# Seven products for eight with w_out also in the first eight tiles of batches 0 to 2, and PSUM in single banks

## The chip, the core and the metric

The kernel runs on one core of a Trainium2 chip. The time is the device time of one execution in microseconds. PE is TensorE's matmul side and PEld its weight loads, DVE is VectorE, ACT is ScalarE, POOL is GpSimd, SP is SyncE, which here only issues DMAs. Each engine works off its own list of instructions in order and waits for others at semaphores.

## What is computed

A long convolution with a gate, then a feed-forward network with a maxout of three (B = 4 batches, S = 12544 positions, D = 128 channels, 768 hidden). Cut to what matters:

```python
h_filt = np.maximum(pos_emb @ w1, 0) @ w2 * window          # (S, D)
u = x * v                                                   # (B, S, D)
y = irfft(rfft(u, 2*S, axis=1) * rfft(h_filt, 2*S, axis=0), axis=1)[:, :S]
t = (x * y).reshape(B * S, D)                               # 50176 tokens
h = np.maximum(np.maximum(t @ moe_w1, t @ moe_w2), t @ moe_w3)
out = h @ moe_w_out
```

All of it is in fp32; each fp32 matmul shows as two MATMUL rows in the profile.

## The kernel before

**Tiles and batches.** S = 128 x 98. A tile is 4 x 98 = 392 tokens, a batch has 32 tiles (NT). The hidden 768 are 6 blocks of 128 (NF), so that a batch's FFN has 192 steps, one for each tile and block. The kernel has four parts: the prologue to about 303 us (the filter's spectrum, the weights, batch 0's forward and inverse transform); the FFNs of batches 0 to 2, each with the next batch's convolution done beside it; the FFN of batch 3, beside which nothing is left to convolve (from about 1860 us on); and the drain.

**The FFN.** `w1` and `w2` are held less `w3`, so that the maxout is `max(relu(a), b)` of two products plus a linear part `lin = w3 @ w_out`. `up` (L721) makes one hidden block of a tile: two products into two of the three banks `hps` (each in two halves of 64 output channels, `halves_mm` at L156), ACT's relu (L727) and DVE's max (L730). `down` (L733) adds that block's product with `w_out` into the bank `ops`, with the product of `lin` first when f is 0; after the sixth block ACT copies the bank (L743) and POOL issues the store (L745). In the loop over tiles a down runs two steps behind its up.

**A tile's input.** `t_load` (L661) has SP fetch the tile's transform (`zt`, four DMAs) and, for every second tile, x (`xT`, four DMAs). `t_sums` (L687) makes a sum and a difference (L696), on POOL while units are in work and on DVE otherwise. `t_last` (L703) does the last transform stage on the PE, in one bank, and DVE multiplies with x (L717); its result `gt` is what the ups read.

**The convolution beside.** `conv_steps(b, done)` plans, for each of the 192 steps, what is added behind the up and the down. First come the 32 units: loads by SP (`u_load`), x * v on DVE (`u_mul`, L361), planes of 16 bit on POOL (`u_planes`, L381 and L382), a transposing DMA issued by SP (`u_dma`, L388), a join on ACT and DVE (`u_join`, L397), and the first transform stage (`u_first`, L413): 32 matmul rows into a double bank, a copy of one half by ACT (`high`, L422) and a sum and a difference by DVE (`spec`, L424). For a unit due at step s these stand at steps s-9, s-6, s-5, s-4, s and s+1; units follow each other every 1.52 steps, and the last are due near step 55 (batch 0) or 62. Then come 45 + 3 quarters: loads by SP (`w_load`, `q_load`, `h_load`), the PE's second and third stages (`g_quarter`, L467 and L477) in one double bank, the copy and sums out of it (`g_fold`, L489 and L492), and the products with the filter's spectrum on ACT, DVE and POOL.

**PSUM.** Eight banks: three `hps`, two double banks `cps` that go round among units, quarters and the turns of tiles (`t_last`), and one `ops`.

**The last batch.** Tiles go in pairs. A pair is taken as a 2 x 2 block product: two tiles (c11 and c12 belong to the first, c21 and c22 to the second) by the two halves of the 768 hidden and the two halves of `w_out`'s 128 columns, and seven products do for eight. A pair has 12 ups, in an order of its own (`ORDER`), the sums s1 to s4 of hidden blocks on POOL (`sum_`, L760, 12 of them of 128 x 392), and seven products (`products`, L790) of which each instruction covers 64 output channels by 196 columns, in two banks X and Y that change places from pair to pair. The results come out by ACT copies and DVE sums (L807) into an `o` tile, and POOL issues its eight stores (L814). Products run nine steps behind the ups (LAG). Five subtractions on DVE (L1175) make the combinations of `w_out` and `lin` that the products use; they stand at the start of the last batch, and one of them overwrites b12 of `w_out`. The order within each engine is the program's own.

Of the kernel before, what the change touches and what calls it, by code (L numbers as in the profile page):

```python
# [91 lines left out]
def kernel(  # L92
# [311 lines left out]
    def u_first(u, i0=0, n=4):  # L404


        t = uts[u] if i0 + n < 4 else uts.pop(u)
        ps = state["bank"]()[:, 0:256 * n]
        at = 4 * u + i0
        for i in range(n):  # L410
            for h in range(2):
                for c in range(2):
                    nc.tensor.matmul(  # L413
                        ps[64 * c:64 * c + 64, 256 * i + h * N1:256 * i + (h + 1) * N1],
                        t[:, 2 * ((at + i) % 8) + h].rearrange("n r t -> n (r t)"),
                        f1q[:, h, c * N1:(c + 1) * N1],
                        start=(i % 2 == 0 and h == 0), stop=True, skip_group_check=True)
        v = ps.rearrange("p (s m) -> p s m", m=256)[:, :, 0:2 * N1].rearrange(
            "p s (h k) -> p h k s", h=2)
        high = cvp.tile([P, n, D], FP32, tag="eo", name="high", bufs=2)  # L420
        high = high[:, :, 0:N1].rearrange("p s k -> p k s")
        nc.scalar.copy(high, v[:, 0])  # L422
        for a, op in enumerate((ALU.add, ALU.subtract)):
            nc.vector.tensor_tensor(out=spec[:, :, a, at:at + n], in0=v[:, 1], in1=high, op=op)  # L424

# [31 lines left out]
    def g_quarter(g, z):  # L457


        ps = state["bank"]()  # L460
        if g is not None:
            w, t = ws.pop((g, 0)), sqs.pop(g)
            for k in range(2):
                for r in range(2):
                    for a in range(2):
                        at = 512 * r + k * D
                        nc.tensor.matmul(  # L467
                            ps[64 * a:64 * a + 64, at:at + D], w[64 * r:64 * r + 64, k, a, :],
                            t[64 * r:64 * r + 64, k, a, :], start=(k == 0), stop=True,
                            skip_group_check=True)  # L470
        if z is not None:
            w, ab = ws.pop((z, 1)), abs_.pop(z)
            for q in range(2):
                for a in range(2):
                    for k in range(2):
                        at = 512 * a + 256 + q * D
                        nc.tensor.matmul(  # L477
                            ps[64 * k:64 * k + 64, at:at + D], w[64 * a:64 * a + 64, k, q, :],
                            ab[64 * a:64 * a + 64, q, k, :], start=(g is None and q == 0),
                            stop=True, skip_group_check=True)  # L480
        pss[g, z] = ps

    def g_fold(g, z):
# [5 lines left out]
        nc.scalar.copy(eo[:, lo:hi], ps[:, 512 + lo:512 + hi])  # L489
        cb = cvp.tile([P, 2, 512], FP32, tag="cb", name="cb", bufs=3)  # L490
        for a, op in enumerate((ALU.add, ALU.subtract)):
            nc.vector.tensor_tensor(out=cb[:, a, lo:hi], in0=ps[:, lo:hi], in1=eo[:, lo:hi],  # L492
# [84 lines left out]
    def conv_steps(b, done):  # L577
# [9 lines left out]
        for u in range(4, done):  # L587
            at(2 * u - 7, 1, u_first, u)
        per_pair = 170 / (NK + LATE + 0.6 * (NU - done))
        for u in range(done, NU):  # L590
# [6 lines left out]
            at(int(s + 1), 1, u_first, u)  # L597
# [29 lines left out]
        for x in range(NK + LATE):  # L627
# [4 lines left out]
            at(s - 4, 0, w_load, x)  # L632
# [4 lines left out]
            if g % 2 == 0:  # L637
                at(s - 4, 0, q_load, g, min(2, NK - g))
# [19 lines left out]
    NT = P // 4  # L658
    zts, xTs, gs, pos_, obs = ({} for _ in range(5))
# [43 lines left out]
    def t_last(i):  # L703
        zt = zts.pop(i)
        ps = state["bank"]()
        own = i[0] == B - 1 and i[1] > 1
        g = (lp if own else hp).tile([D, 4, NB], FP32, tag="g", name="gt", bufs=4 if own else 3)
# [14 lines left out]
    def up(i, f, tag="hid", bufs=3):  # L722
        rhs = gs[i][:].rearrange("d p n -> d (p n)")
        h = (hidp if tag == "hid" else lp).tile([P, N], FP32, tag=tag, name="hid", bufs=bufs)
# [8 lines left out]
    def down(i, f, h):  # L733
        if f == 0:
            pos_[i] = ops.tile([D, 512], FP32, tag="ops", name="ops")
# [26 lines left out]
    def s3(h, j):  # L762
        h["s3", j] = lp.tile([P, N], FP32, tag="s3", name="s3", bufs=3)
        sum_(h["s3", j], h["h11", j], h["h21", j], ALU.subtract)

    def s2(h, j):
        h["s2", j] = lp.tile([P, N], FP32, tag="s2", name="s2", bufs=3)
# [5 lines left out]
    def s4(h, j):  # L773
        sum_(h["h12", j], h["h12", j], h["s2", j], ALU.subtract)

    SUMS = {2: (s3, 0), 4: (s2, 0), 5: (s3, 1), 7: (s3, 2), 8: (s2, 1), 9: (s2, 2),
            10: (s1, 0), 11: (s1, 1), 12: (s1, 2), 13: (s4, 0), 14: (s4, 1), 15: (s4, 2)}

    def products(b, i, h, X, Y):
# [5 lines left out]
        def new(name, bufs=1):  # L785
            return lp.tile([P, H2], FP32, tag=name, name=name, bufs=bufs)
# [6 lines left out]
        def place(name):  # L793
# [5 lines left out]
            if m not in t:  # L799
                t[m] = lp.tile([P, 2, H2], FP32, tag="o", name="o", bufs=2)  # L800
# [8 lines left out]
        def stored(m):  # L809
            dst = outT.rearrange("d (p b n) -> d p b n", b=B, n=NB)  # L810
            for n in range(2):
                for c in range(2):
                    at = 4 * (i + n) + 2 * c
                    nc.gpsimd.dma_start(  # L814
# [8 lines left out]
            (X, "h21", wo_sb[:, 0:NC, 64:128], True, None, [(added, "c22", "u3", X)], None),  # L823
# [16 lines left out]
    def run(steps):  # L840
        for fn, args in steps:
            fn(*args)

# [112 lines left out]
    state = {"cv": (cvp, cps), "xb": 2, "bank": bank,  # L956
# [69 lines left out]
    def unit(u):  # L1026
        for h in range(2):
            u_first(u, 2 * h, 2)

# [52 lines left out]
    nc.sync.dma_start(sign_t[:], sign_d)  # L1082
    op_ = ctx.enter_context(tc.tile_pool(name="op", bufs=2))
    conv = ExitStack()
    inq = conv.enter_context(tc.tile_pool(name="inq", bufs=1))
    wp = conv.enter_context(tc.tile_pool(name="wp", bufs=3))
    hh = conv.enter_context(tc.tile_pool(name="hh", bufs=2))
    cvp = conv.enter_context(tc.tile_pool(name="cvp", bufs=3))
    hps = ctx.enter_context(tc.tile_pool(name="hps", bufs=1, space=PSUM))
    cps = conv.enter_context(tc.tile_pool(name="cps", bufs=1, space=PSUM))  # L1090
    ops = conv.enter_context(tc.tile_pool(name="ops", bufs=1, space=PSUM))
    hbanks = itertools.cycle([hps.tile([P, 512], FP32, name=f"hps{i}") for i in range(3)])
    pairs = itertools.cycle([cps.tile([P, 1024], FP32, name=f"cps{i}") for i in range(2)])
    state = {"bank": lambda: next(pairs)}
# [5 lines left out]
    for n, (b, i) in enumerate(tiles[:LAST]):  # L1100
        if i == 0:
            beside, plan, pairs_from = conv_steps(b + 1, EARLY if b == 0 else 0)
        if n == 0:
# [3 lines left out]
            u_first(2)  # L1107
            t_last(tiles[0])
            u_first(3)
        for f in range(NF):  # L1110

            if i < NT - 2:
                if f == 0:
                    t_load(*tiles[n + 2])
            elif i == NT - 1 and f < 2 and n + 1 + f < len(tiles):
                t_load(*tiles[n + 1 + f])
            turn_ = i == NT - 1
            if f == 4 and n + 1 == LAST:
                t_sums(tiles[n + 2], nc.vector)
            h = up((b, i), f)  # L1120
            for a in range(2):
                if f == plan[i][a]:
                    t_sums(tiles[n + 1],
                           nc.vector if turn_ or i * NF > pairs_from else nc.gpsimd, (a,))
            late.append(((b, i), f, h))
            if len(late) > 2:
                down(*late.pop(0))
            if f == plan[i][2]:
                t_last(tiles[n + 1])
            if f == 5 and n + 1 == LAST:  # L1130
                t_last(tiles[n + 2])
            s = i * NF + f
            run(beside.pop(s, ()))
            if s == NT * NF - 1:
                assert not beside, sorted(beside)
    first = up((B - 1, 0), 0)
    for l in late:
        down(*l)
    conv.close()


    lp = ctx.enter_context(tc.tile_pool(name="lp", bufs=1))
    cps = ctx.enter_context(tc.tile_pool(name="cps2", bufs=1, space=PSUM))
    singles = itertools.cycle([cps.tile([P, 512], FP32, name=f"last{i}") for i in range(3)])
    state = {"bank": lambda: next(singles)}
# [3 lines left out]

    tw = lp.tile([P, 3, NC, 64], FP32, name="tw", bufs=1)  # L1150
    linx = lp.tile([D, 64], FP32, name="linx", bufs=1)
    b11, b12 = wo_sb[:, 0:NC, 0:64], wo_sb[:, 0:NC, 64:128]
    b21, b22 = wo_sb[:, NC:, 0:64], wo_sb[:, NC:, 64:128]
    weights = [(tw[:, 1], b22, b12), (b12, b12, b11), (tw[:, 0], b22, b12),
               (tw[:, 2], b21, tw[:, 0]), (linx[:], lin[:, 0:64], lin[:, 64:128])]

    stream = {}

    def later(step, fn, *args):
        stream.setdefault(step, []).append((fn, args))  # L1160

    step, b = 0, B - 1
    for i in range(0, NT, 2):
        h = {}
        X, Y = banks if i % 4 == 0 else banks[::-1]
        for j, (name, f) in enumerate(ORDER):
            n = int(name[1]) - 1
            if j < 2 and i + 2 < NT:
                t_load(b, i + 2 + j)
            own = (name, BUFS[name]) if step > 2 else ("hid", 3)  # L1170
            h[name, f] = first if step == 0 else up(
                (b, i + n), f + (NC if name[2] == "2" else 0), *own)
            if step > 2 and weights:
                out, a1, a2 = weights.pop(0)
                nc.vector.tensor_tensor(out=out, in0=a1, in1=a2, op=ALU.subtract)  # L1175
            if j == 0:
                entries = products(b, i, h, X, Y)
                for q, e_ in enumerate(entries):
                    at_ = step + LAG + q * NSTEP // len(entries)
                    for fn in e_:  # L1180
                        if isinstance(fn, tuple):
                            later(at_ + 1, *fn)
                        elif fn is not None:
                            later(at_, fn)
                for at_, (fn, c) in SUMS.items():
                    later(step + at_, fn, h, c)
# [45 lines left out]
```

## Time and profile before

| | |
|---|---|
| runs | 2292.55, 2300.68, 2299.49, 2294.06 us; median 2296.78 |
| profiled execution | 2292.55 us, of which the span from the first to the last instruction is 2290.7 |
| granted TensorE clock | 0.999 |
| matmul rows of `up` (392 columns) | 6144 |
| matmul rows of `down` with `w_out` (392 columns) | 2304 |
| POOL sums of hidden blocks, L760 | 192, all in the last batch |
| SP's transposing DMAs, L388, in the profile | 90 |

The page gives busy time by engine, the share of the span in 40 slices, the DMA queues, the chain of work that ended last, and the costliest groups of instructions with what ended the idle time before them. Where a helper issues an instruction, its line is the helper's: ups, downs, lin and turns of tiles are all L156, and are told apart by the names of their tiles (`hps<-gt,w_sb` an up, `ops<-hid,wo_sb` a down, `ops<-gt,lin`, `cps<-f4p,even` a turn). In the timeline a row is a run of like instructions: start, duration, engine, line, operation, tiles, form and count; what stands in brackets is the idle time before it and what ended it. By stage (busy us in windows of the span):

| window, us | what runs | PE | DVE | ACT | POOL |
|---|---|---|---|---|---|
| 845 to 980 | batch 1, units beside | 135.0 of 135 | 94.1 | 62.6 | 56.8 |
| 1000 to 1180 | batch 1, quarters beside | 178.3 of 180 | 141.6 | 115.8 | 56.6 |
| 1900 to 2260 | batch 3, pairs, no convolution | 360.0 of 360 | 173.0 | 91.9 | 233.7 |

### The profile page before, as it was taken

To read this page: it belongs to the slowest core of one execution; us is meant where nothing else is said; L and a number is where in the kernel's file an instruction comes from. 1 tells how busy PE (TensorE), PEld (TensorE's weight loads), DVE (VectorE), ACT (ScalarE), POOL (GpSimd) and SP (SyncE) were. 2 spreads that over 40 slices of the span, in tenths; PEclk is the share of its full clock that TensorE was granted. 3 is DMA by queue.
4 is the path that set the end of the run, shared out by engine and by line. 5 is a ranking of instruction groups with operands and counts; after the bars stand their busy time and mean duration, and the time that the engine had idled before them with its cause. 6 is when DMAs were issued, how large, how long until landed. Compare 5 with 4: busy or idle time off the path is not lost.

```text
span 2290.7 us, 68538 instructions
## 1 busy us (share of the span) xinstructions
PE 2259.0 (99%) x27855; PEld 1372.9 (60%) x27855; DVE 1556.0 (68%) x2848; ACT 1175.7 (51%) x2124; POOL 874.8 (38%) x1093
## 2 busy tenths in 40 slices
PE   8999989999999999999999999999999999999998
PEld 7999856655555556655555556655555556666665
DVE  5588857667878747758887847758887854545443
ACT  2688834456666534456666624446666622222222
POOL 2044423323333234423333324323333326666666
PEclk9999999999999999999999999999999999999999
DMA  7779979799999669969999769969999832222221
GB/s 190 179 238 277 293 166 186 142 216 235 236 238 232 168 147 186 190 153 249 249 236 248 198 129 198 185 148 236 250 252 248 212 86 55 55 66 66 62 55 22
DMA packets 473270, 411.03 MB, mean 179 GB/s; under 512 B 327866, under 2 KB 374427, under 8 KB 472955
## 3 DMA queue, kind: packets, MB, share of 16 engines
q1 hardware_dynamic: 445954, 329.48, 64.7%
q0 software_dynamic: 26288, 75.47, 11.3%
q8 instruction: 219, 3.59, 0.7%
q10 hardware_dynamic: 712, 1.70, 0.3%
q14 instruction: 97, 0.79, 0.1%
HBM read 262.84 MB, written 84.67 MB: 152 GB/s over the span
## 4 chain that ended last, share of the span: by engine, by line
PE 90%; DMA 4%; DVE 3%; issue 1%; ACT 1%; SPq 0%; POOL 0%; DVEq 0%; POOLq 0%; ACTq 0%
PE hps L156 41%; PE ops L156 17%; PE ops L790 6%; PE cps L413 5%; PE cps L156 3%; PE ps L156 3%; PE cps L467 3%; PE ps L165 3%; PE cps L477 2%; PE sps L1000 2%; PE gps L982 1%; DMA wt<-wq_const 1%; PE last L156 1%; DVE xs L523 1%; DMA hd<-ht 1%
## 5 line engine op out<-in xcount | busy, mean ns | idle before, releaser
L156 PE MATMUL hps<-gt,w_sb 128*64 128x392 f32 x6144 | 1148.8, 494 | 0.0
L727 ACT ACTIVATE hid<-hps 128x392 f32<-128x392 f32 x768 | 384.1, 500 | 724.5 <-PE hps L156 709.7
L156 PEld LDWEIGHTS hps<-gt,w_sb 128*64 128x64 f32 x6144 | 427.9, 137 | 423.9 <-issue 395.8
L730 DVE TENSOR_TENSOR hid<-hid,hps 128x392 f32<-128x392 f32 x768 | 428.2, 558 | 341.3 <-PE hps L156 336.1
L156 PE MATMUL ops<-hid,wo_sb 128*64 128x392 f32 x2304 | 479.0, 492 | 0.0
L519 POOL TENSOR_TENSOR cb<-cb,xs 128x512 f32<-128x512 f32 x135 | 174.4, 1292 | 471.3 <-DVE xs L516 352.1
L156 PEld LDWEIGHTS ops<-hid,wo_sb 128*64 128x64 f32 x2304 | 170.0, 137 | 209.2 <-issue 209.2
L424 DVE TENSOR_TENSOR spec<-cps,high 128x360 f32<-128x360 f32 x188 | 141.3, 792 | 127.3 <-ACT high L422 127.3
L492 DVE TENSOR_TENSOR cb<-cps,eo 128x512 f32<-128x512 f32 (+1 forms) x288 | 175.2, 649 | 72.0 <-ACT eo L489 72.0
L745 POOL DMA_DIRECT2D out_dram<-ot x96 | 75.1, 783 | 367.5 <-ACT ot L743 312.6
L507 ACT ACTIVATE xs<-cb 32x512 f32<-32x512 f32 x270 | 169.6, 628 | 19.7 <-DVE cb L492 10.9
L508 ACT COPY xs<-cb 32x512 f32<-32x512 f32 x270 | 166.3, 616 | 3.2
L422 ACT COPY high<-cps 128x360 f32<-128x360 f32 x94 | 75.1, 799 | 164.5 <-PE cps L413 135.7
L523 DVE TENSOR_TENSOR xs<-cb 128x256 f32<-128x256 f32 x270 | 147.8, 594 | 10.9 <-POOL cb L519 10.9
L413 PEld LDWEIGHTS cps<-f1q,uT 98*64 98x64 f32 x3008 | 131.7, 138 | 31.8 <-issue 31.0
L413 PE MATMUL cps<-f1q,uT 98*64 98x90 f32 x3008 | 135.3, 242 | 1.3 <-DVE spec L424 0.5
L382 POOL COPY planes<-ut 128x784 uint16<-128x784 uint16 x90 | 75.8, 842 | 119.0 <-DVE ut L361 118.9
L500 POOL DMA_DIRECT2D zd<-cb x135 | 93.0, 691 | 50.5 <-DVE cb L492 47.4
L156 PEld LDWEIGHTS cps<-f4p,even 90*64 90x64 f32 x1568 | 89.8, 138 | 37.0 <-issue 33.5
L156 PE MATMUL cps<-f4p,zt 90*64 90x49 f32 x1568 | 97.2, 222 | 0.4 <-DVE zt L696 0.4
L156 PE MATMUL cps<-f4p,even 90*64 90x49 f32 x1568 | 95.9, 220 | 1.5 <-DVE even L696 1.5
L814 POOL DMA_DIRECT2D out_dram<-o x128 | 77.6, 611 | 51.7 <-DVE o L807 49.5
(134 smaller groups left out, 3130.0 us busy)
## 6 DMA issues: line engine op xcount, KB each, us to landing
ht<-hd SPq DMA_DIRECT2D x264, 256.0 KB, 7.0
wt<-wq_const SPq DMA_DIRECT2D x144, 256.0 KB, 6.7
zd<-cb POOLq DMA_DIRECT2D x135, 256.0 KB, 6.5
zt<-zd SPq DMA_DIRECT2D x384, 90.0 KB, 3.1
sq<-spec SPq DMA_DIRECT2D x264, 128.0 KB, 7.2
ut<-in_xr_dram SPq DMA_DIRECT2D x128, 196.0 KB, 4.3
ut<-in_vr_dram SPq DMA_DIRECT2D x128, 196.0 KB, 4.5
xT<-in_x_dram SPq DMA_DIRECT2D x256, 98.0 KB, 3.7
```

The costliest lines, as they stand in the source:

```text
L156: nc.tensor.matmul(out[64 * h:64 * h + 64], lhsT[:, 64 * h:64 * h + 64], rhs, start=start, stop=stop, skip_group_check=True)
L413: nc.tensor.matmul(ps[64 * c:64 * c + 64, 256 * i + h * N1:256 * i + (h + 1) * N1], t[:, 2 * ((at + i) % 8) + h].rearrange("n r t -> n (r ...
L424: nc.vector.tensor_tensor(out=spec[:, :, a, at:at + n], in0=v[:, 1], in1=high, op=op)
L492: nc.vector.tensor_tensor(out=cb[:, a, lo:hi], in0=ps[:, lo:hi], in1=eo[:, lo:hi], op=op)
L500: nc.gpsimd.dma_start(zd[b][2 * z:2 * z + 2].rearrange("k c t a f -> (k c t) a f"), zss.pop(z))
L507: nc.scalar.mul(xs[at:at + 32], xt[at + 32:at + 64], -1.0)
L508: nc.scalar.copy(xs[at + 32:at + 64], xt[at:at + 32])
L519: nc.gpsimd.tensor_tensor(out=xts[g], in0=xts[g], in1=xs[:], op=ALU.add)
L523: nc.vector.tensor_tensor(out=ab[:, q], in0=y[:, 0], in1=y[:, 1], op=(ALU.subtract, ALU.add)[q])
L727: nc.scalar.activation(h[:], pa[:, 0:N], Relu)
L730: nc.vector.tensor_tensor(out=h[:], in0=h[:], in1=pb[:, 0:N], op=ALU.max)
L790: nc.tensor.matmul(ps[64 * c:64 * c + 64, 0:H2], w, rhs[:, H2 * c:H2 * c + H2], start=start, stop=True, skip_group_check=True)
```

## The change

**Pairs in batches 0 to 2.** The first eight tiles (TP) of each of these batches are done as four pairs, with the ups, sums and products of the last batch, beside the units. The fourth pair (`ends`) has its product entries drawn together, from step 3 on after the lag, so that the stage ends near step 52. From tile 8 on, steps are as before. While pairs run no `down` is issued in steps 2 to 8 of a batch. Their stores are issued by SP instead of POOL, two steps after the results (one, in the fourth pair); the last batch's stay on POOL. `t_load`, `t_sums` and `t_last` of the pairs' tiles get places of their own, the sums of tiles 2 to 7 on POOL; in batch 0 tile 1's sums are on DVE ahead of the loop and its turn is in step 0. The tile after next is loaded and turned in a batch's last tile.

**Memory.** A pool `stp` holds the hidden blocks and sums of the pairs until their stage ends; only then are the pools of the quarters' `w`, `sq` and `h` opened, so that `w_load` and `q_load` are held back to step 52 (LOADS).

**The weights' combinations** now lie in a `tw` of four matrices, b12 is no longer overwritten, and the five subtractions stand in steps 1 to 5 of batch 0.

**PSUM.** Instead of two double banks there are four single ones (`singles`). While pairs run three of them go round, and the fourth and `obank` (the former `ops`) are the pairs' X and Y; afterwards all four go round, and `obank` is the bank of the downs again. A unit is done in two halves of one bank each; a quarter takes two single banks; a turn of a tile takes one single bank instead of a double one. Tile 8's downs begin in `obank` at step 50.

```diff
+    def unit(u):
+        for h in range(2):
+            u_first(u, 2 * h, 2)
...
-        ps = state["bank"]()
+        ps = [state["bank"]() for _ in range(2)]
...
-            at(int(s + 1), 1, u_first, u)
+            at(int(s + 1), 1, unit, u)
...
-            at(s - 4, 0, w_load, x)
+            at(max(s - 4, LOADS), 0, w_load, x)
...
+    TP = 8
+    LOADS = TP * NF + 4
...
-            pos_[i] = ops.tile([D, 512], FP32, tag="ops", name="ops")
+            pos_[i] = obank
...
-                    nc.gpsimd.dma_start(
+                    sp["store"].dma_start(
...
-            (X, "h21", wo_sb[:, 0:NC, 64:128], True, None, [(added, "c22", "u3", X)], None),
+            (X, "h21", tw[:, 3], True, None, [(added, "c22", "u3", X)], None),
...
+    def down_pair(b, i, h, banks, step, ends, wait):
+
+        entries = products(b, i, h, *banks)
+        for q, e_ in enumerate(entries):
+            at_ = q * NSTEP // len(entries)
+            if ends:
+                at_ = min(at_, 3 + (q > 8) + (q > 13) + (q > 20))
+            at_ += step + LAG
+            for fn in e_:
+                if isinstance(fn, tuple):
+                    later(at_ + wait, *fn)
+                elif fn is not None:
+                    later(at_, fn)
+        for at_, fn, c in SHORT if ends else SUMS:
+            later(step + at_, fn, h, c)
...
+    obank = cps.tile([P, 512], FP32, name="ops")
+    singles = [cps.tile([P, 512], FP32, name=f"cps{i}") for i in range(4)]
+    turn_of = {"at": 0, "of": 4}
...
+    sp = {"hid": ("h11",), "store": nc.sync}
...
+            turns_.close()
+            sp["pool"] = turns_.enter_context(tc.tile_pool(name="stp", bufs=1))
+            turn_of["of"] = 3
...
+            s = i * NF + f
             turn_ = i == NT - 1
...
+            if i < TP:
+                i0, j = i - i % 2, i % 2 * NF + f
+                if j == 0:
+                    h = {}
+                    ends = i0 + 2 == TP
+                if j in (0, 6 if ends else 4):
+                    t_load(b, i0 + 2 + (j > 0))
+                up_pair(b, i0, h, j)
+                if late:
+                    down(*late.pop(0))
+                if n == 0 and f == 0:
+                    t_last(tiles[1])
+                elif weights:
+                    out, a1, a2 = weights.pop(0)
+                    nc.vector.tensor_tensor(out=out, in0=a1, in1=a2, op=ALU.subtract)
+                if j == 0:
+                    banks = (obank, singles[3])
+                    down_pair(b, i0, h, banks if i0 % 4 == 0 else banks[::-1], s, ends,
+                              1 if ends else 2)
...
+            if i < TP and not ends:
+                if j in (3, 7):
+                    t_sums((b, i0 + 2 + (j > 3)))
...
+            run(stream.pop(s, ()))
...
+            if i < TP and not ends:
+                if j in (7, 10):
+                    t_last((b, i0 + 2 + (j > 7)))
...
+            if i >= TP and turn_of["of"] == 3 and not stream:
+                turns_.close()
+                wp = turns_.enter_context(tc.tile_pool(name="wp", bufs=3))
+                hh = turns_.enter_context(tc.tile_pool(name="hh", bufs=2))
+                turn_of["of"] = 4
             run(beside.pop(s, ()))
```

## The prediction

> **What bounds the kernel now.** I read, in this order, the page's busy shares and chain, the waits of the PE in the three batches that have a convolution beside them, the PE's timeline in both kinds of FFN, the busy time by stage, and the rows of the operations that the change touches.
>
> ```profile
> span 2290.7 us, 68538 instructions
> PE 2259.0 (99%) x27855; PEld 1372.9 (60%) x27855; DVE 1556.0 (68%) x2848; ACT 1175.7 (51%) x2124; POOL 874.8 (38%) x1093
> PE 90%; DMA 4%; DVE 3%; issue 1%; ACT 1%; SPq 0%; POOL 0%; DVEq 0%; POOLq 0%; ACTq 0%
> ```
>
> The PE is busy 99% of the span, and 90% of the chain that ended last is PE. From the start of batch 0's FFN to the end of batch 2's (303 to 1860 us) the PE waited 10.5 us in all; the largest entry in its list of waits (total, times, longest) is
>
> ```profile
> PE cps L467 <- DVE gt L717: 6.9, 8, 0.9
> ```
>
> So PE work taken out comes off the time as long as the other engines keep up. What a product costs is read from the PE's timeline, in batch 0 and in the last batch:
>
> ```profile
> 702.98 1.49 PE L156 MATMUL hps<-gt,w_sb 128*64 128x392 f32 x8
> 704.30 0.83 PE L156 MATMUL ops<-hid,wo_sb 128*64 128x392 f32 x4
> 704.96 0.50 PE L156 MATMUL hps<-gt,w_sb 128*64 128x392 f32 x2
> ```
>
> ```profile
> 2104.97 1.49 PE L156 MATMUL hps<-gt,w_sb 128*64 128x392 f32 x8
> 2106.28 0.83 PE L790 MATMUL ops<-hid,wo_sb 128*64 128x196 f32 x8
> 2106.95 1.49 PE L156 MATMUL hps<-gt,w_sb 128*64 128x392 f32 x8
> ```
>
> From start to start, four instructions of 392 columns take 0.66 us and eight of 196 columns 0.67. Averaged over long undisturbed windows I get 164.6 ns for one of 392 and 82.9 ns for one of 196.
>
> **The products (a gain).** A tile has 6 downs and one lin, 7x4 = 28 instructions of 392 columns; a pair 56x164.6 ns = 9.22 us. With seven products a pair has 21 product entries and 4 lin entries of four rows each, 100x82.9 ns = 8.29 us. That is 0.93 us a pair, and 12 pairs (4 in each of batches 0 to 2): **-11.1 us**.
>
> **Moved weights and single banks (small gains).** The five subtractions leave the start of the last batch, where two turns of the PE waited 0.31 and 0.40 us for DVE behind them: **-0.7**. In batch 0 they lie on DVE in steps 1 to 5 (214 to 705 ns each), beside units 4 and 5, in time that DVE has idle (30% in the stage below); without that cover they would cost the 0.7 again. Nine waits of the kind shown above, 7.7 us together, come where the second quarter of a slot wants the double bank that the turn of a tile holds until gt. With singles it still gets that bank as its second one and waits for it some instructions later; I count 0.1 us for each, **-0.8**, with the ends 0 and -7.7. A unit in halves has the same matmuls. Its copies and sums change by these rows (min/median/max):
>
> ```profile
> L422 ACT COPY high<-cps x94: 768/797/816, 303.9 to 1515.5; 128x360 f32<-128x360 f32 x94
> L422 ACT COPY high<-ps x4: 472/495/513, 290.4 to 296.0; 128x180 f32<-128x180 f32 x4
> L424 DVE TENSOR_TENSOR spec<-cps,high x188: 761/792/822, 305.9 to 1517.1; 128x360 f32<-128x360 f32 x188
> L424 DVE TENSOR_TENSOR spec<-ps,high x8: 334/336/347, 293.1 to 296.8; 128x180 f32<-128x180 f32 x8
> ```
>
> ACT gains 2x495-797 = 0.19 us of work a unit, DVE loses 2x792-4x336 = 0.24. Neither sets the pace there:
>
> ```profile
> 845.00:980.00 135.00, 135.00 (x1742) 84.84 (x1740) 94.08 (x165) 62.61 (x109) 56.79 (x81) 1.00 1.08 184
> ```
>
> That is the stage of units: PE 135 of 135 us, DVE 94 (70%), ACT 63 (46%), POOL 57 (42%). Cost nothing; if ACT's idle half were gone it would be 78x0.19 = 15 us.
>
> **The wait for obank (a cost).** Tile 8's first lin goes into obank, which the last pair's products used; the matmul stands in the PE's order behind ups, and it waits for the DVE sum c21. Behind it on the PE are all later ups, and so ACT and DVE too. L807's sum of 128x196 takes 0.353 us; a wait on gt of 0.563 us cost 0.82, so 0.26 lies around an operation; DVE is 70% busy, and a sum or max ahead of it takes 0.3 to 0.8 us. I take 0.8 (ends 0.3 and 1.4), three batches: **+2.4**.
>
> **Batch 0's start (a cost).** Pairs need both tiles at once: tile 1's turn is put in step 0 and its gt is wanted by step 1, with nothing else for the PE. Tile 0's start shows the price, waits of 1.50, 0.40 and 0.55 us, of which the first is
>
> ```profile
> 305.26 0.32 PE L156 MATMUL cps<-f4p,even 90*64 90x49 f32 x4 [1.50 <-DVE even L696]
> ```
>
> I take the sum of those three for tile 1, rounded: **+2.5** (0.5 if DVE's two sums are ready, 4 if ACT's and DVE's halves of units are in their way).
>
> **The starts of batches 1 and 2 (a cost).** No down runs in steps 2 to 8 of a batch, so a step takes 1.32 us instead of 1.98, and the units' first loads, 4.5 us to landing, have 7x0.66 = 4.6 us less before slot 10. The work comes back at the end of the stage; what is lost is only where a unit is late: **+2** for both (0 to 4).
>
> **POOL, SP and the rest of the stage (a cost).** A pair brings 12 sums to POOL and takes away two stores:
>
> ```profile
> L760 POOL TENSOR_TENSOR s<-hid,s x48: 1015/1027/1039, 1874.4 to 2274.1; 128x392 f32<-128x392 f32 x48
> L388 SPq DMA_TRANSPOSE turned<-planes x90: 1231/1284/3398, 322.1 to 1498.1; - x90
> DMA to landing us min/median/max: 3.1/4.4/7.6
> ```
>
> 12x1.02-2x0.78 = 10.7 us in some 36 us of a pair: POOL goes from 42% to about 73%. Its planes for a unit (0.84 and 0.30 us), which the transpose on SP waits for, stand behind one or two sums, 1.0 to 2.0 us. SP gets 8 stores a pair, at 0.45 us like its other loads 3.6 us: 65% to about 77% of its queue. Behind them stand transposes, behind these the join on ACT and DVE, behind that the relu of the next up, and the PE. The cover is the time between a turned tile's landing and its join: from the 90 landings and joins, 0.8 us at the least, 3.1 at the twentieth part, 6.3 in the middle. With 1 to 2 us from POOL and 1.8 (four stores) from SP most units stay covered. I take **+1.5**; ends 0 (all covered) and 16, worked out below. The stores' landing is waited for by nobody soon: the o tile has two turns.
>
> A rule of the Trainium skill speaks against the sums: "SBUF — State Buffer", section "Who interferes with whom", has a DVE instruction with two SBUF inputs contend with a GpSimd instruction that reads SBUF, one holding the shared port until it ends. The trace is divided: L397's copy on DVE has a median of 455 ns and a longest of 1356, while L361's product of two SBUF tiles is 558 in the median, though one of it took 1405. By the rule the two L361 products of 78 units, blocked half a sum (0.5 us) in a third of cases, would cost 26 us of DVE time, as an estimate; by the medians nothing; DVE's idle 30% would take it either way.
>
> **The sum.** -11.1-0.7-0.8+2.4+2.5+2+1.5 = -4.2, on a span of 2290.7 with 1.85 us around it (profiled run 2292.55). That run is the fastest of four, 4.2 us under the median of 2296.78; a rerun has no reason to repeat it, so I put the change on the median: **2292.6 us**. About 0.3%, 6.9 us, is what a measurement of this kernel can tell from no change; this lies inside it.
>
> **Rivals.** *A, the PE stays fed.* Loads were issued early and the singles turn quickly: then the starts cost 0.5 and 0, the stage nothing, and the sum is -11.1-0.7-0.8+2.4+0.5 = -9.7: **2287.1**. For it: a wait of PE on anything but gt is rare before. Against it: batch 0's gaps for tile 0 are in the trace. *B, slower: SP's bursts make the joins late.* A burst is four stores, 1.8 us, in one slot, before that slot's transpose; 8 bursts a batch, 6 beside units, 18 in all, up to 18x1.8 = 32 us, if the cover is gone. It decides from where POOL's delay before the planes plus the burst passes the middle cover of 6.3 us, which needs some four sums in a row ahead of planes; half of the bursts in full is +16, so 2292.6+16 = **2308.6**. For it: the transposes already wait on SP up to 3.2 us behind planes. Against it: the cover at the twentieth part, 3.1, is nearly what one burst and one sum take. *C, the products don't get cheaper beside units*: excluded by 82.9 against 164.6 ns, unless halves of width 196 meet a late operand there; 12x8.29x0.1 = 10 us for a tenth, which would end near 2302. I count it with B.
>
> **Chances.** Forecast 0.37, A 0.35, B and C 0.28. The range of the forecast alone: low all costs at their lower ends (+0.9+0.5+0+0 for +2.4+2.5+2+1.5, so 7 below, 2285.6), high +1.8+1.5+2+3 above, 2300.9. The whole range takes A's lower end with part of the nine waits gone (2284) and B a little past half of its price (2312). Faster by over 0.3% 0.35, within 0.37, slower 0.28.
>
> **What will show it.** Products: L790's rows beside units at 83 ns and the last batch the same length. Obank: a wait of lin's matmul on DVE c21 of about 0.8 us, once a batch. Starts: PE gaps in the first 10 us of each batch. B: ACT's join or high as the releaser of ups, joins close on landings, and PE waits on ACT hid or DVE hid in steps 9 to 52. The prediction is wrong if the PE waits more than some 15 us beside the pairs, or if the second quarter's wait goes entirely (-7).

## The result, and the profile after

The changed kernel takes 2303.09 us in the median of 31 runs, the kernel before 2297.6 in 51: a ratio of 1.0022, 95% interval [1.0015, 1.0028]. It is slower by some 5 us where -4.2 was forecast. Both lie inside the 0.3% that the forecast called no change, on opposite sides of zero. The page of the changed kernel:

```profile
span 2303.1 us, 70310 instructions
PE 2259.3 (98%) x28383; PEld 1423.1 (62%) x28383; DVE 1606.2 (70%) x3102; ACT 1203.6 (52%) x2218; POOL 1019.4 (44%) x1207
PE 62%; DMA 10%; DVE 2%; POOL 2%; SPq 2%; issue 1%; ACT 0%; POOLq 0%; DVEq 0%; ACTq 0%
```

PE's share of the chain went from 90% to 62%: other engines now set when the PE goes on, in many short steps. PE's busy time is no smaller although there are fewer columns to do: ends of matmuls are modelled, and part of the waiting and of a slower clock counts as busy. The waits of the PE from 303 us to the end of batch 2's FFN (total, times, longest):

```profile
PE cps L472 <- DVE gt L728: 5.3, 8, 0.7
PE cps L413 <- DVE uT L397: 3.3, 7, 1.0
PE hps L156 <- DVE hid L741: 2.7, 3, 1.1
PE cps L413 <- DVE spec L425: 2.5, 2, 2.0
...
PE cps L802 <- POOL s L771: 1.5, 2, 0.7
PE ops L156 <- DVE o L819: 1.4, 3, 0.5
PE cps L472 <- DMA wt<-wq_const: 1.2, 3, 0.6
```

All entries together are 22 us, where the kernel before had 11. The wait of second quarters has shrunk (6.9 to 5.3); new are units whose join (uT) or sums (spec) are late, ups that wait for a max, products that wait for POOL. The stage of units, which before had POOL at 57 and DVE at 94 of 135 us:

```profile
845.00:980.00 135.00, 131.73 (x1826) 100.16 (x1824) 107.54 (x237) 69.95 (x136) 106.44 (x122) 1.00 1.03 188
```

POOL is at 79% (forecast 73%), DVE at 80% where I had left its 70%, and the PE has 3.3 us idle where it had none.

Time from one landmark to the next, read off the PE's timeline at the starts of ups, in two profiles of each kernel (the second of each, and the singles, are experiments below), tells where the time went. Step 56 of a batch is just behind its pairs.

| from, to (us) | before | before, again | singles, no pairs | singles, again | changed | changed, again |
|---|---|---|---|---|---|---|
| start to first up | 309.9 | 312.5 | 312.7 | 308.2 | 311.9 | 311.7 |
| batch 0, to step 56 | 160.8 | 162.0 | 160.8 | 159.6 | 162.2 | 160.6 |
| to batch 1's step 56 | 517.5 | 517.5 | 517.4 | 517.4 | 520.7 | 522.4 |
| to batch 2's step 56 | 520.4 | 521.7 | 520.2 | 520.1 | 526.9 | 526.9 |
| to batch 3's first up | 358.3 | 358.0 | 357.5 | 357.8 | 358.8 | 357.5 |
| batch 3, to its last up | 408.3 | 408.3 | 407.5 | 407.5 | 407.3 | 407.3 |

The first three rows of the FFN each hold four pairs, and should have become 3.7 us shorter. They lie between 1.4 us shorter and 6.5 longer. Batch 0's row moves by itself: some profiles begin it with the end of a stretch in which the granted clock is 0.50 (up to 316.1 us, 3.6 us of the row, in the second profile of before), others don't (the second ones of the singles and of the changed kernel).

### The profile page after: what moved, and what is told of

It is laid out like the page before. It is cut to its first block, busy times and chain, and to the rows that moved or that the text cites. A ratio compares the mean times of both kernels' runs of the same rounds, so it can differ in the third digit from the quotient of the medians.

```text
span 2303.1 us, 70310 instructions
## 1 busy us (share of the span) xinstructions
PE 2259.3 (98%) x28383; PEld 1423.1 (62%) x28383; DVE 1606.2 (70%) x3102; ACT 1203.6 (52%) x2218; POOL 1019.4 (44%) x1207
## 4 chain that ended last, share of the span: by engine, by line
PE 62%; DMA 10%; DVE 2%; POOL 2%; SPq 2%; issue 1%; ACT 0%; POOLq 0%; DVEq 0%; ACTq 0%
PE hps L156 33%; PE ops L156 11%; PE ops L802 7%; PE cps L413 3%; DMA zt<-zd 3%; PE cps L156 2%; DMA ht<-hd 2%; PE cps L472 2%; DMA wt<-wq_const 2%; PE cps L482 2%; DMA sq<-spec 2%; PE last L156 1%; PE cps L802 1%; DVE xs L528 1%; POOL s L771 1%
## 5 line engine op out<-in xcount | busy, mean ns | idle before, releaser
L741 DVE TENSOR_TENSOR hid<-hid,hps 128x392 f32<-128x392 f32 x768 | 428.4, 558 | 351.5 <-PE hps L156 341.7
L156 PE MATMUL ops<-hid,wo_sb 128*64 128x392 f32 x1728 | 357.6, 492 | 0.0
L156 PEld LDWEIGHTS ops<-hid,wo_sb 128*64 128x64 f32 x1728 | 124.3, 137 | 159.1 <-issue 159.0
L756 POOL DMA_DIRECT2D out_dram<-ot x72 | 56.6, 786 | 287.6 <-ACT ot L754 231.9
L423 ACT COPY high<-cps 128x180 f32<-128x180 f32 x188 | 91.8, 489 | 150.7 <-PE cps L413 95.8
L425 DVE TENSOR_TENSOR spec<-cps,high 128x180 f32<-128x180 f32 x376 | 109.1, 339 | 42.9 <-ACT high L423 41.0
L771 POOL TENSOR_TENSOR s<-hid 128x392 f32<-128x392 f32 x84 | 95.6, 1139 | 78.7 <-DVE hid L741 52.5
L361 DVE TENSOR_TENSOR ut<-ut 128x392 f32<-128x392 f32 x128 | 90.1, 704 | 31.8 <-DMA ut<-in_vr_dram 28.9
L771 POOL TENSOR_TENSOR s<-hid,s 128x392 f32<-128x392 f32 x84 | 90.8, 1082 | 41.3 <-DVE hid L741 41.0
```

The costliest lines, as they stand in the source:

```text
L156: nc.tensor.matmul(out[64 * h:64 * h + 64], lhsT[:, 64 * h:64 * h + 64], rhs, start=start, stop=stop, skip_group_check=True)
L741: nc.vector.tensor_tensor(out=h[:], in0=h[:], in1=pb[:, 0:N], op=ALU.max)
L771: nc.gpsimd.tensor_tensor(out=out[:], in0=a[:], in1=b[:], op=op)
```

## The experiments

Ratios are to the kernel before, run on the same chip, with 95% intervals; the changed kernel's is 1.0022.

**Single banks without pairs (e1_singles, and e14_singles_again).** The whole change but the pairs.

```diff
-    TP = 8
-    LOADS = TP * NF + 4
+    TP = 0
+    LOADS = 0
...
```

> No pairs in batches 0 to 2: all their tiles go as before, with the stores on POOL, but PSUM in single banks, units in halves and the weights' subtractions in batch 0, as in the changed kernel. All theories agree that the losses of the changed kernel lie in the stage of pairs: they expect 2 to 4 us under the kernel before (0.999 to 0.998), from the waits of second quarters (9 x 0.2 us and more) and the last batch's 1 us. A rival, that single banks or halves are what costs, expects this run 5 us or more above the kernel before.

Measured: 2290.97 us, 0.9976 [0.9966, 0.9987], and once more 2290.33 us, 0.9968 [0.9956, 0.9981]. Single banks, halves and moved weights are together a gain, 6 to 7 us, larger than any theory had it (which of the three gives it wasn't tested); the pairs are worth +11 to +13 us. The profiles account for about half of the gain: from the first up to batch 3's last, the singles' two take 3.4 us less than the two of before in the mean, of which nine second quarters are 0.2 us each and batch 3 is 0.8 us. The rest is open.

**No sums on POOL (e2_no_sums).**

```diff
     def s1(h, j):
+        if sp["store"] is nc.sync:
+            return
```

The like stands in s2, s3 and s4.

> The 12 sums of hidden blocks per pair on POOL are left out in batches 0 to 2: the products read the hidden blocks without them, so that the output of those tiles is another. Lock theory (POOL's sums hold up DVE's copy of a join, 455 ns before and 668 to 1138 in the middle now, and take POOL's time from the planes): the waits of the PE on units, some 9 us, and part of the two starts go; 8 to 11 us under the changed kernel, 0.997 to 0.998 of the kernel before. Queue theory (SP's stores are what makes joins late): 0 to 3 us under the changed kernel.

Measured: 2291.46 us, 0.9979 [0.9968, 0.9991], 10 us under the changed kernel. Of the join's copies on DVE, here are the rows of the changed kernel and then of this one (min/median/max):

```profile
L397 DVE COPY uT<-turned x90: 446/826/3126, 333.4 to 1523.7; 98x512 uint16<-98x512 uint16 x90
```

```profile
L397 DVE COPY uT<-turned x90: 445/453/1544, 331.4 to 1511.8; 98x512 uint16<-98x512 uint16 x90
```

The copy took 455 ns before, 826 beside sums, and 453 again without them. That is the lock that the lock theory supposes, shown by taking away its cause. The products x * v on DVE (L361), which I had looked at for it, kept their median (558, 559, 559), and that median hides the same lock: of the 90 beside the FFNs, the changed kernel has 41 that overlap no sum or difference of POOL, at 539 to 569 ns, and 49 that do, at 938 in the mean and up to 3150. In the kernel before only 3 of the 90 met one. DVE's maxes (L741), which read one operand from PSUM, took 543 to 565 ns whether they met one or not. The 10 us are not the lock alone, for without the sums POOL's queue is shorter too.

**No stores of pairs (e3_no_stores).**

```diff
         def stored(m):
+            if b < B - 1:
+                return
```

> The stores of the pairs in batches 0 to 2 are left out, so that the output of those tiles isn't written. Queue theory (bursts of four stores, 2.6 us on SP's queue, make transposes late, and these the joins): the PE's waits on units go, 6 to 10 us under the changed kernel. Lock theory: 0 to 3 us under it.

Measured: 2293.73 us, 0.9987 [0.9978, 0.9996], 8 us under the changed kernel: what queue theory expected. SP's queue in the changed kernel:

```profile
1403.31 2.67 SPq L826 DMA_DIRECT2D out_dram<-o  x4
1406.15 3.70 SPq L388 DMA_TRANSPOSE turned<-planes  x2
1409.90 0.59 SPq L354 DMA_DIRECT2D ut<-in_xr_dram  x1
1410.53 1.44 SPq L354 DMA_DIRECT2D ut<-in_vr_dram  x1
1412.02 2.57 SPq L826 DMA_DIRECT2D out_dram<-o  x4
1414.63 0.59 SPq L354 DMA_DIRECT2D ut<-in_xr_dram  x1
```

SP has next to no gap here, and four stores take 2.6 us, not the 1.8 that I had worked out. The loads behind them are late as well: from 303 to 1530 us DVE waited 1.9 us for loads of v before, 14.5 in the changed kernel and 2.3 without stores. The time between a turned tile's landing and its join, 6.3 us in the middle and 3.1 at the twentieth part before, was 5.2 and 0.4 in the changed kernel, 6.0 and 1.3 without stores. Both theories hold, then: either edit alone takes most of the loss away. That a join late by one cause has no cover left for the other would explain it, and is argued, not shown.

**Both copies of a join on ACT (e4_join_act).**

```diff
-            copies[h](
+            nc.scalar.copy(
```

> Both copies of a join are on ACT, none on DVE; 0.77 us more for ACT a unit, 0.67 us or more less for DVE. Lock theory: the join no longer waits for POOL's sums, and the PE's waits on DVE's uT go (3.3 us in the profile), with some of those on the sums of units behind it: 3 to 6 us under the changed kernel. Queue theory: within 2 us of it, since late transposes make the joins as late on ACT; a loss of 2 us or more if ACT's longer join holds up relus.

Measured: 2297.73 us, 1.0002 [0.9992, 1.0012], 4.6 us under the changed kernel, the expected size. The waits on DVE's uT (3.3 us) are gone; those on spec are 4.2.

**The two kernels once more (e5_before_again, e6_after_again).**

> The kernel before once more, unchanged, for a second profile. The run with single banks alone was 6 us under it, of which its profile explains some 3 (second quarters, the last batch). If the rest is the state of the one profile of before (the fastest of its runs), a second profile lies 2 to 5 us above 2290.7, in the prologue or in waits of the PE on units; if it repeats the first within 1 us, the double banks cost something that the profile doesn't show.

> The changed kernel once more, unchanged. Waits at fixed places (starts of batches 1 and 2, tile 8's lin, batch 0's first quarters) repeat within 0.3 us each; those on units move, and with them the stretch of halved clock.

Measured: spans of 2295.6 and 2301.8 us. The profile that I predicted from was one with a quick prologue (2.6 us of the difference) and no waits on the quarters' loads, of which the second has 1.0 us. In the changed kernel the spacing of matmuls at the starts of batches 1 and 2 exceeds the normal by 1.29 and 0.89 us, at tile 8 by 0.61, as in the first to 0.02; the units' waits moved: those on spec grew from 2.5 to 5.1 us, those on DVE's uT fell from 3.3 to 1.3.

**Stores on ACT (e7_stores_act), and with both join copies on ACT (e8_stores_and_join_act).**

```diff
-    sp = {"hid": ("h11",), "store": nc.sync}
+    sp = {"hid": ("h11",), "store": nc.scalar}
```

> The pairs' stores of batches 0 to 2 are issued by ACT instead of SP; the lock by POOL's sums stays. If SP's queue is the cause, the time falls as far as without stores, less what ACT's issues (8 a pair) cost: 5 to 9 us under the changed kernel (0.998 to 1.000 of the kernel before). If the stores' traffic and not their place in SP's queue was the cost, within 2 us of the changed kernel.

> Stores on ACT and both copies of a join on ACT: both mended causes at once. If queue and lock are two causes that add up, 10 to 14 us under the changed kernel (0.996 to 0.998); if they are one (a join is late by one or the other), no further than the better of the two alone, 6 to 9 us.

Measured: 1.0005 [0.9996, 1.0014] and 0.9983 [0.9974, 0.9993]. The first is 4 us under the changed kernel, half of what leaving the stores out gave; how much of the other half is ACT's time and how much the transfers', it doesn't tell. Together they give 9 us. That is what was expected of one cause, but also the sum of the two edits alone (3.9 and 4.6), since the first gave less than expected: this pair of runs doesn't decide it.

**Early loads (e9_loads_early).** This run and those behind it build on e8.

```diff
+            if done or u > 2:
+                at(max(0, int(s) - 9), 0, u_load, b, u)
...
+                if turn_ and f > 2 and b + 2 < B:
+                    u_load(b + 2, f - 3)
```

> As the run with stores and both join copies on ACT, and the loads of the first three units of batches 1 and 2's convolution partners are issued in the last three steps of the batch before. In that run the PE still waits about 1.3 us for DVE and 0.7 us for POOL's sum some 15 us into batches 1 and 2, where DVE sits behind a unit's product whose load is late. If the short steps 2 to 8 outrun the loads, the 1.3 us go in both batches: 2 to 3 us less (0.9970 to 0.9975 of the kernel before). If SP or the planes hold the units at the start, they stay, and the time is the same within 1 us.

Measured: 0.9981 [0.9972, 0.9990], 0.4 us less than the run before it, and the 1.3 us stay. These lines show why, of SP, POOL and DVE in this run's timeline:

```profile
829.66 1.75 SPq L680 DMA_DIRECT2D zt<-zd  x4
840.58 0.40 SPq L354 DMA_DIRECT2D ut<-in_xr_dram  x1
```

```profile
838.19 1.35 POOL L772 TENSOR_TENSOR s<-hid,s 128x392 f32<-128x392 f32 x1
...
839.72 0.83 POOL L382 COPY planes<-ut 128x784 uint16<-128x784 uint16 x1
```

```profile
844.73 1.15 DVE L361 TENSOR_TENSOR ut<-ut 128x392 f32<-128x392 f32 x1 [2.48 <-DMA ut<-in_vr_dram]
845.79 1.02 DVE L742 TENSOR_TENSOR hid<-hid,hps 128x392 f32<-128x392 f32 x2
```

SP is idle from 831.4 us: the next load waits for its buffer, which the planes of an earlier unit release. These stand on POOL behind sums of tiles and of hidden blocks and end at 840.55; the load goes out at 840.58. DVE reaches that unit's product too early, waits 2.48 us in front of it, and two maxes stand behind.

**All places (e10_all_places), stores apart (e11_stores_apart), products later (e12_products_later).** In e10 the fourth pair's last entries stand ahead of tile 8's lin, and batch 0's start is reordered; e11 puts the second four stores a step later and the first units' x * v a step later; e12 does the latter for all units.

```diff
-                at_ = min(at_, 3 + (q > 8) + (q > 13) + (q > 20))
+                at_ = min(at_, 3 + (q > 8) + (q > 13))
...
-                    later(at_ + wait, *fn)
+                    later(at_ + wait + (ends and fn[1]), *fn)
...
-            at(int(s) - 6, 0, u_mul, u)
+            at(int(s) - 5, 0, u_mul, u)
```

> As the run before it, with two more places mended: the last four product entries of the fourth pair stand one step earlier, ahead of tile 8's lin, so that other matmuls cover the DVE sum that lin waits for (0.61 us in each of three batches); and in batch 0 tile 1's sums stand ahead of unit 3, and units 4 and 5 one step earlier, so that a unit covers tile 1's gt (0.58 and 0.85 us waits there). By the waits 2.5 to 3.5 us less than the run before it. If the products' gain is all there and only the listed waits are left, it ends 6 to 9 us under the run with single banks alone less what units still cost: 0.995 to 0.9965 of the kernel before.

> As the run with all places mended, whose eight stores of a fourth pair came in one step and held ACT for 6.1 us and the PE for 2 to 3.4: now the second four stand a step behind the first. In batches 1 and 2 the products x * v of the first eight units stand a step later on DVE, behind another max, so that DVE no longer waits there for a late load. If the eight stores are what that run lost by, its waits at steps 51 and 52 go and the 1.3 us at the starts too: 8 to 11 us under it (0.995 to 0.997 of the kernel before), under the run with single banks alone. If the mended places only move the wait, it stays above 0.998.

> The same with the products x * v of all units a step later. If late loads hold DVE throughout the stage of pairs (14.5 us of DVE's waits in the changed kernel), 1 to 2 us less than the run with the first eight alone; if the slack between landing and join is what is short, 1 to 3 us more, with waits of the PE on ACT's uT.

Measured: 1.0029 [1.0019, 1.0039], 0.9986 [0.9977, 0.9994], 0.9977 [0.9967, 0.9988]. In e10 the waits on lin and the first ones at batch 0's start went, and a larger one came, three times; the timeline of ACT, with its queue, then of the PE:

```profile
976.40 6.08 ACTq L827 DMA_DIRECT2D out_dram<-o  x8
982.53 1.40 ACT L397 COPY uT<-turned 98x512 uint16<-98x512 uint16 x2 [5.64 <-DMA out_dram<-o]
```

```profile
983.98 1.86 PE L413 MATMUL cps<-f1q,uT 98*64 98x90 f32 x32 [3.39 <-ACT uT L397]
```

Eight stores in one step hold ACT for 6 us, and the join behind them. Apart, the waits there are 0.7 us at most, and e11 is 9.9 us better, though not under the singles. e12 is 2.1 us better still, a step that the intervals don't separate; DVE's waits for loads of v fell from 12.6 to 2.7 us, so the late loads did hold DVE.

**Tile sums on DVE (e13_tile_sums_dve).** e12 still had 4.3 us of PE waiting for POOL's sums, 1.8 at a time in batches 1 and 2, where a tile's sums stand ahead of the hidden blocks'.

```diff
-                    t_sums((b, i0 + 2 + (j > 3)))
+                    t_sums((b, i0 + 2 + (j > 3)), nc.vector if b and i0 == 0 and j == 7 else nc.gpsimd)
```

> As the run with all products x * v a step later, and in the first pair of batches 1 and 2 tile 3's sums are on DVE instead of POOL, where they stood just ahead of two sums of hidden blocks. If POOL's queue is what the second product of these pairs waits for (1.8 us, twice), those waits go and the profiled time after the first up falls by 3 to 4 us; 0.9955 to 0.9965 of the kernel before, 3 us under the run with single banks alone. If DVE is then late instead (it locks against POOL's sums), the time stays within 1.5 us.

> The run with single banks and no pairs once more, on the same chip as the run before it, to compare the two directly: 0.997 to 0.9985 of the kernel before.

Measured: 0.9965 [0.9951, 0.9979], 2289.59 us, beside 0.9968 for the singles on the same chip. The POOL wait is gone (4.3 to 0.6 us), but 1.4 us of waiting for DVE's max came back, and the profiled time after the first up fell by 1.7 us, half of the expected. Where the rows of the table above hold pairs, this run has 158.0, 516.0 and 518.6 us, 4.5 in all under the singles' second profile, taken beside it: 4.5 us of the 11.1 are out. (Under the first it would be 5.8, but that one has 2.3 us at half clock in batch 0's row.) That the whole run is better than the singles by as much isn't shown; the medians lie 0.7 us apart, inside the intervals, and the time before the first up alone varied from 308.2 to 314.8 us between profiles.

## Why the prediction was wrong, point by point

**Products: right.** Rows of 196 columns beside units came at 83 ns from start to start, and the work taken out is the 11.1 us.

**Weights, halves and banks: right in kind, too small.** Second quarters waited 1.8 us less (forecast 0.8) and batch 3 took 1.0 less (0.7). The whole part was -6 to -7 us, not -1.5, of which the profiles explain half. This miss hid a part of the other: with -1.5 the changed kernel would have ended near 2308 us, about where rival B put it.

**The wait for obank: right.** 0.61 us by start-to-start spacing, three times, 1.8 instead of 2.4. The PE's timeline at tile 8 of batch 0:

```profile
458.18 0.88 PE L156 MATMUL ops<-gt,lin 128*64 128x392 f32 x4 [0.45 <-DVE o L819]
```

**Batch 0's start: right.** Its gaps, 0.58, 0.85 and 0.66 with smaller ones, are some 2.3 us (2.5), and some 3 in the second profile.

**Starts of batches 1 and 2: mechanism partly right, price too low.** 1.28, 0.88 and 0.38 us in each, 5.0 for 2. I had the loads late because steps are short. e9 shows for the first of the three that POOL's sums in front of the planes are the reason, by way of a buffer. The second is a product that waits for POOL's sum itself, and went with the tile sums in e13.

**POOL, SP and the rest of the stage: the step that failed.** "I take +1.5" came to some 12 to 15. By the table the changed kernel takes 12.7 us more than the singles from batch 0's first up to batch 3's, though 11.1 us of work are out: 23.8 us of delay, of which 1.8 are the wait for obank, 2.3 batch 0's start and 5.0 the starts of batches 1 and 2; 14.7 are left. The PE's timeline shows where. Between 316 and 1866 us the spacing of matmuls, start to start, exceeds what the same matmuls usually take by 19 us more in the changed kernel than in the singles, if the larger delays alone are counted (22 to 23 with the small ones): 8.1 of it ahead of units' matmuls (0.7 at the starts), 4.6 ahead of ups, 2.3 ahead of quarters, 1.8 each at tile 8 and ahead of products that wait for POOL. Less tile 8's and the starts' that is 12.

Rival B had a part of the mechanism, SP's bursts. The point from which it decides was set too high: I let a delay count only from the middle cover, 6.3 us, while the twentieth part of the units had 3.1 or less, and one burst with a sum or two takes that up; four stores took 2.6 us instead of 1.8; and the delays do not stay on one queue. SP late makes the load late (e3), DVE stands in front of its product, and the maxes behind it are late too. The sign that I had named, over 15 us of waiting beside the pairs, came: some 21 us by the spacing.

The place where it is dearest shows the last term that the sum lacked. The timelines of DVE, then of the PE, in the changed kernel:

```profile
1462.57 1.30 DVE L397 COPY uT<-turned 98x512 uint16<-98x512 uint16 x1
1466.18 0.57 DVE L361 TENSOR_TENSOR ut<-ut 128x392 f32<-128x392 f32 x1 [2.32 <-DMA ut<-in_vr_dram]
...
1469.72 0.57 DVE L361 TENSOR_TENSOR ut<-ut 128x392 f32<-128x392 f32 x1 [1.75 <-DMA ut<-in_vr_dram]
1470.20 1.09 DVE L425 TENSOR_TENSOR spec<-cps,high 128x180 f32<-128x180 f32 x4
```

```profile
1468.11 0.84 PE L413 MATMUL cps<-f1q,uT 98*64 98x90 f32 x16 [0.53 <-DVE uT L397]
1470.94 1.47 PE L413 MATMUL cps<-f1q,uT 98*64 98x90 f32 x16 [1.98 <-DVE spec L425]
1472.16 2.86 PE L156 MATMUL hps<-gt,w_sb 128*64 128x392 f32 x8
```

The spec sums, which free a bank, stand on DVE behind two products whose loads are late; the unit's second half waits for that bank; and behind a wait of 1.98 us the same eight matmuls take 2.86 us instead of 1.5. The windows show the granted clock (PEclk, the third number from the end) at 0.51:

```profile
1470.00:1476.00 6.00, 5.06 (x32) 3.36 (x34) 3.43 (x11) 2.12 (x4) 3.81 (x5) 0.51 1.11 235
1478.00:1490.00 12.00, 12.00 (x193) 9.47 (x190) 8.23 (x21) 6.46 (x13) 7.70 (x10) 1.00 0.75 141
```

Five busy microseconds at half clock cost some 2.5 us on top of the wait, and the stretch goes on to 1476.9 us, some 3 us in all. The Trainium skill's page "TensorE: Matmul & The Clock Gate", section "Part 1: The HAM clock gate", has the gate go to half after an idle window of about 3.4 us; here two waits of 0.53 and 1.98 us with half a unit between them were enough.

**The rule on shared ports: nearer than my reading of the trace.** The Trainium skill's page "SBUF — State Buffer", section "Who interferes with whom", also names copies, when their operands meet its conditions; the join's copy is one, and slowed down beside the sums (453 to 826 ns). I weighed the rule on the products x * v alone and took their median in the kernel before as evidence against it, where only 3 of 90 had met a sum. In the changed kernel the 49 that met one took some 19 us of DVE's time more. (My estimate of 26 counted two products for each unit; there is one.) The joins' copies took another 38. Then I said that DVE's idle 30% would take it, which was wrong in kind: DVE works in order, and what the lock costs is not its share of DVE's time but its delay of the unit behind it. Taking the join's copy off DVE gave 4.6 us (e4).

**The base: right.** The profiled run was the fastest of four, and the median that I took instead, 2296.78, held (2297.6 in 51 runs). e5 shows that its prologue was 2.6 us quick, and that a second profile has waits in the quarters that the first hadn't.

## What to carry to other kernels

When an engine off the critical path gets work, the question is not its new share but which of its instructions others wait for, and what now stands in front of these; take the short end of the spread of slack, not its middle, and follow a delay over all the queues that it crosses. Before putting sums on POOL beside DVE work, look which DVE instructions are copies from SBUF to SBUF or take two SBUF tiles: those that met a sum took nearly twice their time here, and the maxes, with one operand in PSUM, took no more than alone. A median over instructions of which most never meet the other engine says nothing of the lock; sort them by overlap. An edit that comes along (here the single banks) is worth a run by itself; it was the gain, and the named part of the change the loss.

## What the runs showed of the hardware that was not expected

A DVE copy of 98x512 took 453 ns without POOL's sums of hidden blocks beside it and 826 in the median with them, up to 3126; a product of two SBUF tiles took 555 where it met no sum of POOL and 938 in the mean where it did; a max with one operand in PSUM took 543 to 565 either way. POOL's sums went from 1.02 us to 1.06 to 1.14 in the mean of each kind, the last batch's, which have no copies beside them, included. The granted clock fell to half for 3.4 or 6.8 us at a time: behind waits of 0.53 and 1.98 us in the changed kernel, of 2.52 us at the same place in its second profile, and of 0.56 and 1.05 us in e2 (0.50 from 1461.2 to 1464.6 us); in e12 two waits of 1.8 us for a POOL sum did not bring it down. A store of the pairs held SP's queue for 0.61 us in the median, and ACT's for 0.76 each in a row of eight.
